# Attention and GELU layer on one core: left-over values between the first two score chunks, normalizations ahead of the sums, the last four pairs' values in the score banks

## The chip, the cores and the metric

The kernel runs on one core of a Trainium2 chip. Times are device microseconds of one execution; most executions of one kernel agree within some tenths of a per cent, this one scatters more. TensorE (PE) multiplies matrices into PSUM banks, VectorE (DVE) copies, adds and multiplies elementwise, ScalarE (ACT) takes exponentials, GpSimd (POOL) here issues transfers (and does six small instructions at the start), and SyncE (SP) issues stores and transposing transfers. A run is called slow when it took over 1.5% longer than the fastest run of the same kernel in its set; all other runs are of the fast state, and means of times are taken over these alone. Where a median or a range includes a slow run, it is said.

## The reference

```python
scores = scale * np.matmul(q, k.transpose(0, 1, 3, 2))        # 8 batches, 12 heads, 448 rows, 64 wide
m = np.max(scores, axis=-1, keepdims=True)
e = np.exp(scores - m)
attn = e / (np.sum(e, axis=-1, keepdims=True) + np.exp(-m) + 1e-09)
x = np.matmul(attn, v)              # then heads side by side: 3584 tokens x 768
h = x @ w_in                        # 768 x 2048
g = 0.5 * h * (1.0 + erf(h * inv_sqrt2))
out = g @ w_out                     # 2048 x 768
```

448 rows are three chunks of 128 and 64 left-over rows. Two heads make a pair, six pairs a batch, 48 pairs in all.

## The kernel before

Attention of later batches is woven into the two layers of earlier ones. A `step` brings the scores of one pair; in every second step (`two`) also the values of two earlier pairs; then some layer items (`work`), each of them a chain of accumulating matmuls into one bank. `ps_bank` has two banks for values and layer items alike, `ps_st` three tiles of two banks for scores.

```python
def values(g, first=True):                   # 6 matmuls, 128 rows x 64 columns of the array
    ...
    if first:
        po_t[g] = ps_bank.tile([P, 512], FP32, name="bank")
    ...
def values_left(*pairs):                     # left-over rows: 2 matmuls per pair, 64 x 64
    ...
def normalize(g):                            # VectorE: reads the pair's bank, frees it
    nc.vector.tensor_tensor(
        out=xt_t[b][:, c, :], in0=po_t.pop(g)[:, 0:S], in1=rec_t.pop(g), op=ALU.mult)

def step(s, work, late=False):
    ...
    two = s % 2 == 0 and s - 3 in et_t
    if two:
        values(s - 4)
    if s < NSTEP:
        for j in range(NK):
            scores(s, j)                     # 4 matmuls each, 64 x 64
    if two:
        values_left(s - 4, s - 3)
        normalize(s - 4)
        values(s - 3, first=False)
        normalize(s - 3)
    add_up(len(sums))                        # what is left of the denominators' additions (VectorE)
    if s < NSTEP:
        sums.extend(presum_items(s))         # 6 more
    for i, f in enumerate(work):
        ...                                  # a layer item, its copy out of the bank on VectorE
        if len(work) < 4:
            add_up((2, 4)[len(work) == 1] if i < 2 else 0)
        else:
            add_up((0, 2, 1, 1)[i])
```

The second half of batch 2's q and k is put in order by four VectorE copies into the tile `hbuf`, from which transposing transfers read; `hbuf` is later layer 1's output of batch 1. That is called after the step `r == 3` of the first batch, hence ahead of the next step's normalizations:

```python
if b == 0 and r in (-1, 3):
    c0 = 0 if r < 0 else NPAIR // 2
    for w in range(2):
        order_by_pairs(2, w, c0, c0 + NPAIR // 2)      # copies on VectorE
        transpose_on_dma(2, w, c0, c0 + NPAIR // 2)
```

The left-over rows come in four transfers per tensor and batch (`load_left`), issued by GpSimd. After the last step the last two pairs still have to go through values, denominators and normalization:

```python
load_table(SET_GELU)
values(NSTEP - 2)
values_left(NSTEP - 2, NSTEP - 1)
normalize(NSTEP - 2)
values(NSTEP - 1, first=False)
normalize(NSTEP - 1)
for f in take(2):                            # two layer-2 items, then layer 1 of the last batch
    f()
```

The softmax here doesn't subtract the row's maximum and nothing guards it: scores larger than these inputs give would overflow.

## Time and profile before

| what | before |
|---|---|
| time, median of the first 3 runs | 427.51 us (423.76 to 432.69, the highest a slow run) |
| span of the profiled run | 426.0 us |
| TensorE busy | 402.2 us (94%) |
| TensorE waits for a normalization (L414) | 6.1 us in 12 |
| TensorE waits for the last quarter of `w_out` | 4.2 us, once |
| mean clock granted to TensorE | 0.995 |

Waits are read from a list "who waited for whom: total, times, longest". An engine counts as waiting only while no instruction of its own is drawn as running. The lines themselves are in the prediction.

GpSimd's issues at the start, by start and duration:

```profile
1.99 2.63 POOL L126 DMA_DIRECT2D klraw<-in_k_dram  x4 [0.68 <-DVE oneb L180]
...
6.76 2.53 POOL L126 DMA_DIRECT2D vl<-in_v_dram  x4
...
12.87 0.72 POOL L97 DMA_DIRECT2D rawq<-in_q_dram  x1
```

Each left-over transfer occupies GpSimd 0.63 us; the first transfer of batch 1 is issued at 12.87.

### The profile page before, as it was taken

How to read it: one execution, taken by the hardware profiler on the slowest of the kernel's cores; microseconds unless marked ns; L12 is line 12 of the kernel's file. 1: busy time of each engine (PE TensorE's matmuls, PEld its weight loads, DVE VectorE, ACT ScalarE, POOL GpSimd, SP SyncE). 2: the span in 40 equal slices, each digit the busy share in tenths (PEclk: the TensorE clock that was granted, in tenths of full speed). 3: DMA queues.
4: the chain of work that ended last, by engine and by line, in shares of the span. 5: the costliest groups of instructions: out<-in, count | busy, mean ns of one | idle time of the engine just before them, and what ended most of it. 6: DMA issues, size and time to landing. Idle time of an engine off the chain costs nothing.

```text
span 426.0 us, 10972 instructions
## 1 busy us (share of the span) xinstructions
PE 402.2 (94%) x4679; PEld 260.9 (61%) x4679; DVE 199.8 (47%) x478; ACT 299.9 (70%) x450; POOL 123.7 (29%) x173
## 2 busy tenths in 40 slices
PE   6788997799999999999999999999999999999996
PEld 3345864455666666566566666656576566677785
DVE  4796435576165712575155732566056731530021
ACT  5999889397987756988687766898688676634300
POOL 8842541286540582045500563030000000000000
PEclk9999999899999999999999999999999999999999
DMA  9999999999991998169921999139011010110022
GB/s 136 149 181 204 199 176 154 194 185 164 142 113 57 143 182 69 39 102 178 114 57 39 158 143 92 58 87 155 20 38 50 27 38 2 58 38 20 2 75 74
DMA packets 137249, 43.81 MB, mean 103 GB/s; under 512 B 118320, under 2 KB 137200, under 8 KB 137200
## 3 DMA queue, kind: packets, MB, share of 16 engines
q0 software_dynamic: 92016, 22.39, 58.0%
q1 hardware_dynamic: 44400, 20.10, 25.8%
q8 instruction: 36, 0.59, 0.6%
q10 hardware_dynamic: 784, 0.62, 0.6%
q14 instruction: 13, 0.11, 0.1%
HBM read 45.61 MB, written 11.01 MB: 133 GB/s over the span
## 4 chain that ended last, share of the span: by engine, by line
PE 74%; DMA 14%; DVE 5%; POOL 3%; issue 2%; ACT 0%; DVEq 0%
PE bank L230 63%; DMA vn<-in_v_dram 5%; DMA w_in_sb<-in_moe_w_in_dram 5%; PE st L327 4%; PE bank L376 3%; DMA w_out_sb<-in_moe_w_out_dram 3%; PE st L398 2%; PE st L230 2%; DMA rawq<-in_q_dram 2%; DVE xt L414 1%; DVE ksum L361 1%; DVE osb L479 1%; DVE t L361 1%; POOL rawk L97 1%; POOL klraw L126 1%
## 5 line engine op out<-in xcount | busy, mean ns | idle before, releaser
L230 PE MATMUL bank<-xt,w_in_sb 128*64 128x448 f16 x1536 | 151.7, 353 | 1.2 <-DVE xt L414 1.1
L315 ACT ACTIVATE et<-st,expb 128x896 f16<-128x896 f32 x144 | 134.3, 1002 | 26.1 <-PE st L327 25.9
L230 PEld LDWEIGHTS <-w_in_sb 128*64 128x64 f16 x1536 | 96.2, 110 | 52.2 <-issue 5.7
L230 PE MATMUL bank<-w_out_sb,gt_odd 128*64 128x384 f16 x1024 | 88.3, 326 | 1.2 <-DVE xt L414 1.1
L479 DVE COPY osb<-bank 128x384 f32<-128x384 f32 x56 | 31.2, 558 | 123.9 <-PE bank L230 123.9
L230 PEld LDWEIGHTS <-gt_odd 128*64 128x64 f16 x1024 | 64.9, 110 | 22.9 <-issue 4.8
L230 PE MATMUL bank<-w_out_sb,gt_even 128*64 128x384 f16 x768 | 69.5, 329 | 8.0 <-DMA w_out_sb<-in_moe_w_out_dram 4.2
L230 PEld LDWEIGHTS <-gt_even 128*64 128x64 f16 x768 | 48.5, 110 | 26.9 <-issue 13.2
L414 DVE TENSOR_TENSOR xt<-bank,rec 128x448 f16<-128x448 f32 x48 | 28.8, 621 | 65.0 <-PE bank L391 61.5
L438 ACT ACTIVATE gt_odd<-bank 128x448 f16<-128x448 f32 (+1 forms) x74 | 29.2, 394 | 23.9 <-PE bank L230 22.8
L315 ACT ACTIVATE el<-st,expb 128x448 f16<-128x448 f32 x48 | 30.7, 640 | 19.2 <-PE st L398 19.2
L442 DVE COPY hbuf<-bank 128x448 f32<-128x448 f32 x54 | 33.6, 622 | 16.5 <-PE bank L230 15.7
L327 PE MATMUL st<-tqk 64*64 64x448 f16 x576 | 38.8, 362 | 2.4 <-ACT et L315 1.5
L113 POOL DMA_DIRECT2D rawq<-in_q_dram x40 | 30.7, 773 | 31.7 <-DMA vn<-in_v_dram 17.7
L361 DVE TENSOR_TENSOR ksum<-ksum,el 64x448 f16<-64x448 f16 x96 | 37.0, 385 | 2.2
L376 PE MATMUL bank<-et,vn 128*64 128x448 f16 x288 | 36.6, 361 | 0.2 <-DVE tqk L250 0.2
L97 POOL DMA_DIRECT2D vn<-in_v_dram x11 | 10.3, 933 | 90.0 <-PE bank L376 89.7
L361 DVE TENSOR_TENSOR ksum<-t,et 128x448 f16<-128x448 f16 x96 | 34.0, 384 | 1.0 <-ACT et L315 0.8
L361 DVE TENSOR_TENSOR t<-et 128x448 f16<-128x448 f16 x96 | 33.1, 386 | 1.6 <-ACT et L315 0.8
L438 ACT ACTIVATE gt_even<-bank 128x384 f16<-128x384 f32 x34 | 16.7, 491 | 21.5 <-PE bank L230 21.5
L405 ACT ACTIVATE rec<-st,oneb 128x448 f32<-128x448 f32 x42 | 26.8, 640 | 4.7 <-PE st L398 4.7
L408 ACT ACTIVATE rec<-rec 128x448 f32<-128x448 f32 x48 | 27.6, 577 | 1.5
(55 smaller groups left out, 266.1 us busy)
## 6 DMA issues: line engine op xcount, KB each, us to landing
vn<-in_v_dram POOLq DMA_DIRECT2D x6, 576.0 KB, 10.5
rawq<-in_q_dram POOLq DMA_DIRECT2D x40, 84.0 KB, 7.6
rawk<-in_k_dram POOLq DMA_DIRECT2D x32, 96.0 KB, 6.1
w_in_sb<-in_moe_w_in_dram POOLq DMA_DIRECT2D x4, 768.0 KB, 15.9
w_out_sb<-in_moe_w_out_dram POOLq DMA_DIRECT2D x4, 768.0 KB, 14.7
out_dram<-osb SPq DMA_DIRECT2D x16, 168.0 KB, 2.2
out_dram<-osb SPq DMA_DIRECT2D x16, 144.0 KB, 2.1
out_dram<-osb SPq DMA_DIRECT2D x16, 120.0 KB, 2.0
```

What stands on the lines that cost most here:

```text
L113: nc.gpsimd.dma_start(out=dst[:, :, j, e, :], in_=view[j, e])
L230: nc.tensor.matmul(out[x], lhs[:, x], rhs, start=start, stop=stop)
L315: nc.scalar.activation(out=out, in_=in_, func=AF.Exp, bias=expb, scale=scale)
L327: nc.tensor.matmul(st[cols, e, 0:S], kt[r, j, cols], qt[r], start=True, stop=True)
L361: nc.vector.tensor_tensor(out=dst, in0=a, in1=x, op=ALU.add)
L376: nc.tensor.matmul(po_t[g][e * D:(e + 1) * D, 0:S], v_t[b][:, 2 * c + e, j, :], et[:, 2 * j + e], start=(first and j == 0), stop=(not firs ...
L405: nc.scalar.activation(out=rec_t[g], in_=den_t.pop(g)[:, 0:S], func=AF.Ln, bias=oneb, scale=1.0)
L408: nc.scalar.activation(out=rec_t[g], in_=rec_t[g], func=AF.Exp, scale=-1.0)
L414: nc.vector.tensor_tensor(out=xt_t[b][:, c, :], in0=po_t.pop(g)[:, 0:S], in1=rec_t.pop(g), op=ALU.mult)
L438: nc.scalar.activation(out=dst[:, 0, :], in_=ph[:, c0:c1], func=AF.Gelu)
L442: nc.vector.tensor_copy(out=h_t[b][:, fc, :], in_=ph[:, 0:S])
L479: nc.vector.tensor_copy(out=osb, in_=po[:, 0:NHW])
```

## The change

It means to let VectorE free the value banks before TensorE needs them, to take the end's two waits away, and to shorten the stream of transfers that the start hangs on. Its core (renamed arguments cut):

```diff
 def load_left(tiles, src, b):          # batch 0: 2 transfers in place of 4
+    n = 2 if b else 1
+    for i in range(n):
...
 def step(s, work, late=False, then=None):
-    if two:
-        values(s - 4)
-    if s < NSTEP:
-        for j in range(NK):
-            scores(s, j)
-    if two:
-        values_left(s - 4, s - 3)
-        normalize(s - 4)
-        values(s - 3, first=False)
-        normalize(s - 3)
-    add_up(len(sums))
+    if s == NSTEP:
+        add_up(len(sums))
+        for g in (s - 4, s - 2):
+            st = ps_st.tile([P, 2, 512], FP32, name="st")
+            for i in range(2):
+                values(g + i, bank=st[:, i])
+        values_left(*range(s - 4, s))
+        normalize(s - 4)
+        normalize(s - 3)
+    else:
+        if two:
+            values(s - 4)
+        for j in range(NK):
+            scores(s, j)
+            if two and j == 0:
+                values_left(s - 4, s - 3)
+        if two:
+            normalize(s - 4)
+            values(s - 3, first=False)
+            normalize(s - 3)
+    if then:
+        then()                         # the reordering copies, now behind the normalizations
+    add_up(2 if two and len(work) > 3 else len(sums))
...
+            if s % 2 and i == len(work) - 1:
+                pass                   # leave the rest of the sums to the next step
-            if len(work) < 4:
+            elif len(work) < 4:
                 add_up((2, 4)[len(work) == 1] if i < 2 else 0)
             else:
-                add_up((0, 2, 1, 1)[i])
+                add_up((2, 2, 2, 0)[i] if two else (0, 2, 1, 1)[i])
...
-load_left(kl_raw, k, 2)
+nc.vector.memset(kl_raw[0], 0.0)
 ...                                    # q, k of batch 2; first half of w_out
+load_left(kl_raw, k, 2)
...
 load_table(SET_GELU)
-values(NSTEP - 2)
-values_left(NSTEP - 2, NSTEP - 1)
 normalize(NSTEP - 2)
-values(NSTEP - 1, first=False)
 normalize(NSTEP - 1)
```

More of the change, by code (lines that the diff above doesn't have):

```diff
@@ L113, in load_pairs, with left_rows @@
                 nc.gpsimd.dma_start(out=dst[:, :, j, e, :], in_=view[j, e])
-    def left_rows(c, e):
-        x = (c + e) % 2
+    def left_rows(b, c, e):
+        x = (c + e) % 2 if b else e
         return slice(x * LEFT, (x + 1) * LEFT)
     def load_left(tiles, src, b):
-        view = src[b, :, NFULL:S].rearrange("(c i e) s d -> i e s c d", i=2, e=2)
-        for i in range(2):
+        tile_, rows = tiles[b % 2], src[b, :, NFULL:S]
+        n = 2 if b else 1
+        for i in range(n):
+            dst = tile_.rearrange("p (c i) x -> p i c x", i=n)[:, i]
+            view = rows.rearrange("(c i e) s d -> i e s c d", i=n, e=2)[i]
             for e in range(2):
-                dst = tiles[b % 2].rearrange("p (c i) x -> p i c x", i=2)[left_rows(i, e), i]
                 x = slice(e * D, (e + 1) * D) if src is k else slice(0, D)
-                nc.gpsimd.dma_start(out=dst[:, :, x], in_=view[i, e])
+                nc.gpsimd.dma_start(out=dst[left_rows(b, i, e), :, x], in_=view[e])
     def load_q(b, *heads):
@@ L358, in add @@
             else:
-                r = left_rows(g % NPAIR, e)
+                r = left_rows(*divmod(g, NPAIR), e)
                 dst, a, x = sum_t[g][r, e], sum_t[g][r, e], el_t[g][r]
@@ L366, in presum_items, with values @@
         return items
-    def values(g, first=True):
+    def values(g, first=True, bank=None):
         b, c = divmod(g, NPAIR)
@@ L372, in values @@
         if first:
-            po_t[g] = ps_bank.tile([P, 512], FP32, name="bank")
+            po_t[g] = ps_bank.tile([P, 512], FP32, name="bank") if bank is None else bank
         for j in range(NK):
@@ L389, in values_left @@
             for e in range(2):
-                r = left_rows(c, e)
+                r = left_rows(b, c, e)
                 nc.tensor.matmul(
@@ L523, in add_up, with step @@
         del sums[:n]
-    def step(s, work, late=False):
+    def step(s, work, late=False, then=None):
         def middle():
@@ L633, with fetch_half @@
     add_up(4)
+    def fetch_half(b, i):
+        c0 = i * NPAIR // 2
+        for w in range(2):
+            order_by_pairs(b, w, c0, c0 + NPAIR // 2)
+            transpose_on_dma(b, w, c0, c0 + NPAIR // 2)
     def fetch(b, r):
@@ L639, in fetch @@
             load_left(vl, v, b + 2)
-        if b == 0 and r in (-1, 3):
-            c0 = 0 if r < 0 else NPAIR // 2
-            for w in range(2):
-                order_by_pairs(2, w, c0, c0 + NPAIR // 2)
-                transpose_on_dma(2, w, c0, c0 + NPAIR // 2)
+        if b == 0 and r == -1:
+            fetch_half(2, 0)
         elif b and r in (0, 1) and b + 2 < B:
@@ L665 @@
                 n = 2
-            step(s, take(n), late=(s == NSTEP or r == (2 if b else 0)))
+            step(s, take(n), late=(s == NSTEP or r == (2 if b else 0)),
+                 then=(lambda: fetch_half(2, 1)) if (b, r) == (0, NPAIR - 2) else None)
         if b == 0 and r == 0:
```

## The prediction

> **What bounds the kernel now.** I read the page's busy table first, then the list of waits of TensorE, then the timeline around the longest of them, and last the windows around the one gap that a transfer makes.
>
> ```profile
> PE 402.2 (94%) x4679; PEld 260.9 (61%) x4679; DVE 199.8 (47%) x478; ACT 299.9 (70%) x450; POOL 123.7 (29%) x173
> ```
>
> TensorE is occupied for 402.2 of 426.0 us; no other engine is near. The change neither adds nor removes a matrix multiplication, so what it can win lies in the 23.8 us in which TensorE stands still, and in what switching between kinds of multiplication costs. The waits of TensorE say who owns those gaps:
>
> ```profile
> PE bank L230 <- DVE xt L414: 6.1, 12, 1.0
> PE bank L230 <- DMA w_out_sb<-in_moe_w_out_dram: 4.2, 1, 4.2
> PE st L327 <- ACT et L315: 1.5, 3, 0.5
> PE bank L187 <- DVE klraw L174: 1.3, 1, 1.3
> ```
>
> The columns are the total, the number of waits and the longest. Twelve times the layer matmuls (L230) wait for VectorE's normalization (L414), which has to empty one of only two accumulator banks; once they wait 4.2 us for a quarter of the second weight matrix. The list restricted to 82 to 370 us gives 4.1 us in 9 waits of the first kind, and after 370 us 1.6 us in 2 (0.80 and 0.81); the twelfth, 0.38 us, lies before the transfer's wait. One typical gap in order of time (start, duration):
>
> ```profile
> 89.50 0.73 PE L376 MATMUL bank<-et,vn 128*64 128x448 f16 x6
> 89.71 0.56 DVE L479 COPY osb<-bank 128x384 f32<-128x384 f32 x1 [1.32 <-PE bank L230]
> ...
> 90.16 0.76 PE L327 MATMUL st<-tqk 64*64 64x448 f16 x12
> 90.30 0.69 DVE L361 TENSOR_TENSOR t<-et 128x448 f16<-128x448 f16 x2
> ...
> 90.76 0.36 PE L391 MATMUL bank<-el,vl 64*64 64x448 f16 x4
> 90.91 0.69 DVE L361 TENSOR_TENSOR ksum<-t,et 128x448 f16<-128x448 f16 x2
> ...
> 91.05 0.76 PE L376 MATMUL bank<-et,vn 128*64 128x448 f16 x6
> ...
> 91.51 1.15 DVE L414 TENSOR_TENSOR xt<-bank,rec 128x448 f16<-128x448 f32 x2
> ...
> 92.18 1.33 PE L230 MATMUL bank<-xt,w_in_sb 128*64 128x448 f16 x12 [0.38 <-DVE xt L414]
> ```
>
> The left-over values (L391) end by about 91.1, so the first normalization could start there; four additions (L361) stand ahead of it on VectorE and it starts at 91.51. Its bank is free at 92.13, while TensorE had been done with its own work since about 91.80. That is the 0.38 us.
>
> **The transfer.** The windows show the 4.2 us wait (engines' busy time, clock granted, share of the DMA engines, GB/s):
>
> ```profile
> 71.00:72.00 1.00, 1.00 (x16) 0.68 (x13) 0.97 (x4) 1.00 (x3) 0.00 (x0) 1.00 1.33 183
> 73.00:74.00 1.00, 0.00 (x0) 0.00 (x0) 0.00 (x0) 1.00 (x2) 0.00 (x0) 1.00 2.93 66
> 77.00:78.00 1.00, 1.00 (x11) 0.74 (x9) 0.00 (x0) 0.00 (x0) 0.00 (x0) 0.58 1.43 237
> 79.00:80.00 1.00, 1.00 (x12) 0.23 (x12) 0.97 (x4) 0.00 (x0) 0.00 (x0) 0.50 1.60 192
> ```
>
> TensorE stops at 72.25 and resumes at 76.43, and from 77 to 80.5 it gets half its clock, which costs about 1.65 us more: value, score and left-over work that takes 0.66 and 0.60 us elsewhere takes 1.31 and 1.06 here, and the rest of the layer item 0.5 us more. So all that TensorE gains before 72 us is lost again in a longer wait, unless the weights land earlier. That makes three stretches with different rules: up to 76 us (set by transfers), 76 to 369 us (TensorE and the banks), and the end.
>
> **What the Trainium skill says.** "PSUM — Partial Sum Buffer", section "PSUM bank collisions raise a hardware error", wants each bank guarded by semaphore against a second engine: the layer matmul really must wait until the normalization has read its bank. The trace agrees: TensorE resumes at 92.18, 0.05 us after the read ends. The same page, "Engine vs sequencer instructions", calls VectorE's queue strict FIFO; so additions issued earlier hold the normalization back, as the 0.4 us from 91.1 to 91.51 shows. "TensorE: Matmul & The Clock Gate", Part 1, has the clock halved after an idle window of about 3.4 us; here 4.18 us of idling brought it to 0.50 for about 3.4 us. "TensorEngine Tiling (Array Packing)", "Key Properties", says that changing the tiling mode drains TensorE: before each switch between 128*64 and 64*64 the weight loads of this trace idle 0.20 to 0.36 us. Scores and left-over values are both 64*64.
>
> **The change part by part.**
>
> 1. Left-over values move between the first and the second score chunk. Nothing is added: 4 matmuls of 0.29 us are done 8 score matmuls (8/12 of 0.60 = 0.40 us) earlier, in the same tiling mode, so no new switch. The normalization can begin about 0.4 us earlier. The price: the second bank is wanted earlier, after 0.66 us of values and 0.20 us of scores, 0.86 us after the last layer item. Above, the copy that frees it ends at 90.27, 0.77 us after 89.50. It fits, with 0.1 us to spare; where the copy is of 448 columns (mean 622 ns against 558) it is about even.
>
> 2. VectorE normalizes ahead of the sums: the instruction order of the changed kernel has the two normalizations straight after the copy, and the four t and ksum additions (4 x 0.3 us) behind them. With 1, the first normalization starts at about 90.75 in the example and ends at 91.4, against 91.80 when TensorE wants the bank: 0.4 us of slack in place of a 0.38 us gap. The postponed additions (up to 6, about 2.1 us) end some 3.1 us after the values, near the end of the first layer item (2.6 us); the copy of that item may come 0.1 to 0.5 us later, but its bank is wanted only after another item. The same move takes the four reordering copies (1.80 us, 80.38 to 82.1) from in front of the normalization at 82.03, where the gap was 1.02 us. So parts 1 and 2 take all 9 gaps from 82 to 370 us: 4.1 us.
>
> 3. The last four pairs. In the kernel before, two pairs of values run at 369.39 and two at 375.05, with these lines at the end:
>
> ```profile
> 376.33 1.04 ACT L408 ACTIVATE rec<-rec 128x448 f32<-128x448 f32 x2
> 376.94 1.16 DVE L414 TENSOR_TENSOR xt<-bank,rec 128x448 f16<-128x448 f32 x2 [1.48 <-ACT rec L408]
> 377.62 5.39 PE L230 MATMUL bank<-w_out_sb,gt_even 128*64 128x384 f16 x64 [0.81 <-DVE xt L414]
> 382.81 18.35 PE L230 MATMUL bank<-xt,w_in_sb 128*64 128x448 f16 x192
> ```
>
> From 369.39 to 382.81 are 13.42 us. Afterwards: 24 value matmuls in a row at the 98.8 ns that the 448-column layer matmuls take (151.7/1536), 2.4 us; 8 left-over ones, 0.55; three layer items at 2.6 us (the distance of the last osb copies), 7.8; four denominator matmuls, 0.4; a switch, 0.2. That is 11.35, or 2.1 us less: both gaps (1.6) and about 0.5 of switching. The score banks are free: their exponentials end near 369.0. The reciprocals of the last pairs, ready some 2.2 us after the denominators, lie beside 5.2 us of layer work.
>
> 4. Batch 0's left-over rows are fetched in 2 transfers instead of 4, for keys and for values. A transfer costs GpSimd 0.63 us to issue, so its stream runs 1.3, then 2.5 us ahead. Up to 13 us GpSimd issues without a break while the DMA engines move 136 GB/s; from 26 to 42 us they move 205. The early stretch is thus partly bound by issuing (small rows account for the rest), and I take some two thirds of 2.5 us: the last weight quarter lands 1.6 us earlier, at 74.8. The move of the next keys' left-over rows behind two weight quarters changes no bytes ahead of the last quarter. The new zeroing (0.38 us) lies before 76 us. TensorE will arrive about 1 us earlier, still wait over 3 us, and still lose its clock.
>
> Sum: 4.1 + 2.1 + 1.6 = 7.8 us; 427.5 - 7.8 = 419.7 us, or 1.8%.
>
> **The rivals.** (a) Transfers bound the early part fully: the DMA share is 1.24 from 4 to 13 us and 1.27 from 26 to 42, no lower, which speaks for it; a transfer of q issued at 9.28 that landed in 3.2 us speaks against. Then part 4 gives nothing: 421.3. (b) The weights land 2.5 us or more earlier and the wait falls well below the clock's window: 0.9 us and the 1.65 us of slow clock come on top, 417. The dip to 66 GB/s at 73 us shows that this landing is a matter of luck; it probably makes most of the spread from 423.8 to 432.7 of the kernel before. (c) A new wait replaces the old: the left-over values for their bank (0.1 us of slack), at up to 20 pair steps by 0.1 to 0.2 us, so 2 to 4 us given back, 422 to 423. (d) ScalarE becomes the bound: it idles 1.58 and 1.9 us once in a pair of steps and loses 0.4 of that; I see no room for it. Nothing points to a slower kernel.
>
> **Range and chances.** Half the uncertainty is the landing of the weights with the clock (0 to 4 us), half is rival (c) and the scatter of runs. 8 in 10: 415.5 to 424. A gain of 2% needs 8.55 us; I expect 7.8 with a spread of about 3 between kernels' means. Faster 0.42, within 2% 0.57, slower 0.01.
>
> **What would show it.** Right: the wait of L230 for L414 falls from 6.1 us to under 0.5; the additions follow the normalizations; 24 value matmuls stand in a row near the end and the layer matmuls after them have no gap; one wait for the weight transfer remains, ending at 74 to 75.5, with a dip of the clock behind it. Wrong: a wait of L391 for a copy into osb or hbuf, in each pair step; a weight wait that ends at 76 or later (part 4 void) or is gone (gain above 9 us); a gain after 82 us that differs from 6.2 us by more than 1.

## The result, and the profile after

| | before | after |
|---|---|---|
| time, median of 4 runs | 427.59 us (423.76 to 432.69, one of them slow) | 414.42 us (412.71 to 414.82) |
| mean of the fast runs | 426.3 us (3 runs) | 414.1 us (4 runs) |
| span of the profiled run | 426.0 | 410.9 |
| mean clock of that run | 0.995 | 1.000 |

Ratio of the fast runs: 0.9713, 95% interval 0.9642 to 0.9784: faster, by 2.9%, and below the range that was forecast. (A ratio here is the mean time of one kernel's fast runs over that of the other's of the same rounds, so not quite the ratio of the medians quoted.) In the changed kernel the line numbers are 3 higher: L233 are the layer matmuls, L417 the normalizations, L445 and L482 the copies out of layer banks. TensorE's busy time and its waits afterwards:

```profile
PE 396.3 (96%) x4679; PEld 245.0 (60%) x4679; DVE 199.8 (49%) x479; ACT 299.6 (73%) x450; POOL 121.1 (29%) x169
```

```profile
PE bank L241 <- DVE xt L417: 1.7, 3, 0.6
PE bank L233 <- DMA w_out_sb<-in_moe_w_out_dram: 1.5, 1, 1.5
...
PE bank L233 <- DVE hbuf L445: 0.5, 1, 0.5
```

The 6.1 us of L230 for L414 have no counterpart. The wait for weights is 1.5 us in place of 4.2. One wait is new: layer 1 of batch 1 for a copy into `hbuf`. And TensorE's busy time fell by 5.9 us although the number of matmuls is the same, 4679. Some 1.6 us of that is the slow clock of the kernel before, which stretched matmuls (worked out below); the rest is a first sign that "busy" contained waiting.

The pair step that the prediction shows, in the changed kernel (start, duration, in order of time):

```profile
82.35 0.73 PE L379 MATMUL bank<-et,vn 128*64 128x448 f16 x6
82.58 0.56 DVE L482 COPY osb<-bank 128x384 f32<-128x384 f32 x1
...
83.22 0.36 PE L394 MATMUL bank<-el,vl 64*64 64x448 f16 x4
...
83.69 0.62 DVE L417 TENSOR_TENSOR xt<-bank,rec 128x448 f16<-128x448 f32 x1 [0.55 <-PE bank L394]
...
83.89 0.76 PE L379 MATMUL bank<-et,vn 128*64 128x448 f16 x6
...
84.48 1.34 PE L233 MATMUL bank<-xt,w_in_sb 128*64 128x448 f16 x12
84.76 0.62 DVE L417 TENSOR_TENSOR xt<-bank,rec 128x448 f16<-128x448 f32 x1 [0.45 <-PE bank L379]
```

From the first value matmul to the first layer matmul: 84.48 - 82.35 = 2.13 us; before, 92.18 - 89.50 = 2.68. VectorE now waits for TensorE (0.55 us for the left-over values), not the other way round. No copy is late for the left-over matmuls: L394 stands in no line of the waits.

The wait for the last weight quarter, in windows (busy time of the engines, then clock, share of the DMA engines and GB/s at the end of the line):

```profile
70.00:71.00 1.00, 0.57 (x8) 0.22 (x3) 0.57 (x2) 1.00 (x2) 0.00 (x0) 1.00 1.39 201
71.00:72.00 1.00, 0.00 (x0) 0.00 (x0) 0.00 (x0) 1.00 (x3) 0.00 (x0) 1.00 1.46 192
72.00:73.00 1.00, 0.88 (x12) 0.77 (x13) 0.00 (x0) 0.91 (x2) 0.00 (x0) 1.00 1.40 251
```

TensorE resumes at 72.12, not 76.43, and its clock stays at 1.00. At the start GpSimd is ahead:

```profile
1.99 1.46 POOL L129 DMA_DIRECT2D klraw<-in_k_dram  x2 [0.68 <-DVE oneb L183]
...
5.55 1.37 POOL L129 DMA_DIRECT2D vl<-in_v_dram  x2
...
10.40 0.79 POOL L97 DMA_DIRECT2D rawq<-in_q_dram  x1
```

And the end is closed:

```profile
356.67 2.44 PE L379 MATMUL st<-et,vn 128*64 128x448 f16 x24
...
359.03 0.57 PE L394 MATMUL st<-el,vl 64*64 64x448 f16 x8
...
359.53 2.79 PE L233 MATMUL bank<-w_out_sb,gt_even 128*64 128x384 f16 x32
...
362.54 5.37 PE L233 MATMUL bank<-w_out_sb,gt_even 128*64 128x384 f16 x64
...
367.74 14.54 PE L233 MATMUL bank<-xt,w_in_sb 128*64 128x448 f16 x152
```

Two traces can be subtracted stretch by stretch. From 426.0 to 410.9 are 15.1 us:

| stretch | us less | how read |
|---|---|---|
| up to TensorE's resuming after the weights | 4.3 | 76.43 to 72.12 |
| resumed item and the pair step behind it | 2.8 | 1.84 + 4.44 us to 1.29 + 2.17 |
| 8 later pair steps with a listed wait | 4.4 | each 2.68 to 2.13 |
| 9 later pair steps without a listed wait | 1.7 | each 2.33 to 2.14 |
| last values to the last batch's layer 1 | 2.35 | 13.42 to 11.07 |
| new wait for `hbuf` | -0.5 | at 87.87 |

These add up to 15.05. The 2.8 are about 1.6 us of slow clock and 1.2 us of bank wait.

**The wait that the list does not show.** In nine pair steps of the kernel before TensorE had no listed wait, and yet they became shorter. One of them:

```profile
113.48 0.76 PE L376 MATMUL bank<-et,vn 128*64 128x448 f16 x6
113.59 1.39 DVE L414 TENSOR_TENSOR xt<-bank,rec 128x448 f16<-128x448 f32 x2 [9.60 <-PE bank L391]
...
114.27 1.98 PE L230 MATMUL bank<-w_out_sb,gt_odd 128*64 128x384 f16 x22
```

The first of two normalizations, 0.62 us each, runs from 113.59 to 114.21; the layer matmul starts 0.06 us later, just as in the listed cases. Six value matmuls are issued in 0.59 us (the distance in the changed kernel, 83.89 to 84.48) but drawn for 0.76, as each is drawn 0.35 us long and they overlap. A wait of 0.2 us lies under their tail.

### The profile page after: what moved, and what is told of

Same layout as the page of the kernel before. It is cut to its first block, busy times and chain, and to the rows that moved or that the text cites. A ratio compares the mean times of both kernels' runs of the same rounds, so it can differ in the third digit from the quotient of the medians.

```text
span 410.9 us, 10968 instructions
## 1 busy us (share of the span) xinstructions
PE 396.3 (96%) x4679; PEld 245.0 (60%) x4679; DVE 199.8 (49%) x479; ACT 299.6 (73%) x450; POOL 121.1 (29%) x169
## 4 chain that ended last, share of the span: by engine, by line
PE 81%; DMA 14%; POOL 3%; issue 1%; DVE 1%
PE bank L233 65%; DMA w_out_sb<-in_moe_w_out_dram 10%; PE st L330 6%; PE bank L379 6%; DMA rawk<-in_k_dram 4%; PE st L401 2%; PE st L233 2%; PE bank L394 1%; POOL vn L97 1%; POOL rawq L97 1%; PE st L379 1%; POOL vl L129 0%; POOL klraw L129 0%; POOL rawk L97 0%; DVE klraw L177 0%
## 5 line engine op out<-in xcount | busy, mean ns | idle before, releaser
L233 PE MATMUL bank<-xt,w_in_sb 128*64 128x448 f16 x1536 | 151.9, 353 | 0.5 <-DVE hbuf L445 0.5
L233 PEld LDWEIGHTS <-w_in_sb 128*64 128x64 f16 x1536 | 93.5, 110 | 54.5 <-issue 3.8
L233 PE MATMUL bank<-w_out_sb,gt_odd 128*64 128x384 f16 x1024 | 88.0, 326 | 0.0
L482 DVE COPY osb<-bank 128x384 f32<-128x384 f32 x56 | 31.2, 557 | 103.2 <-PE bank L233 103.1
L233 PEld LDWEIGHTS <-gt_odd 128*64 128x64 f16 x1024 | 57.8, 110 | 27.6 <-issue 2.1
L233 PE MATMUL bank<-w_out_sb,gt_even 128*64 128x384 f16 x768 | 68.5, 327 | 1.5 <-DMA w_out_sb<-in_moe_w_out_dram 1.5
L417 DVE TENSOR_TENSOR xt<-bank,rec 128x448 f16<-128x448 f32 x44 | 27.5, 624 | 76.1 <-PE bank L394 63.5
L233 PEld LDWEIGHTS <-gt_even 128*64 128x64 f16 x768 | 43.2, 110 | 23.8 <-issue 4.9
L330 PE MATMUL st<-tqk 64*64 64x448 f16 x576 | 41.6, 358 | 2.5 <-ACT et L318 1.5
L445 DVE COPY hbuf<-bank 128x448 f32<-128x448 f32 x54 | 33.5, 620 | 10.8 <-PE bank L233 8.9
L97 POOL DMA_DIRECT2D vn<-in_v_dram x11 | 10.5, 955 | 88.1 <-PE bank L379 85.9
L379 PE MATMUL bank<-et,vn 128*64 128x448 f16 x264 | 33.0, 356 | 0.2 <-DVE tqk L253 0.2
L330 PEld LDWEIGHTS <-tqk 64*64 64x64 f16 x576 | 15.2, 105 | 23.1 <-issue 18.7
```

Of the source, the lines that this page charges most:

```text
L97: nc.gpsimd.dma_start(out=tiles[b][:, h0:h1], in_=src[b, h0:h1, 0:n * nj].rearrange("h (p j) d -> p h j d", j=nj),)
L233: nc.tensor.matmul(out[x], lhs[:, x], rhs, start=start, stop=stop)
L330: nc.tensor.matmul(st[cols, e, 0:S], kt[r, j, cols], qt[r], start=True, stop=True)
L379: nc.tensor.matmul(po_t[g][e * D:(e + 1) * D, 0:S], v_t[b][:, 2 * c + e, j, :], et[:, 2 * j + e], start=(first and j == 0), stop=(not firs ...
L417: nc.vector.tensor_tensor(out=xt_t[b][:, c, :], in0=po_t.pop(g)[:, 0:S], in1=rec_t.pop(g), op=ALU.mult)
L445: nc.vector.tensor_copy(out=h_t[b][:, fc, :], in_=ph[:, 0:S])
```

## The experiments

Two letters tell the starting point: `a_` is the changed kernel with something undone, `b_` the kernel before with something added. Times are medians; each run is compared with runs of the kernel before on the same chip (424 to 432 us, medians 425.75 to 428.01; of these 43 runs two, at 431.52 and 432.37, were slow). The results were correct except in the two runs where a wrong result was meant. Two theories stood against each other for the 5 us more than forecast. Theory 1: the pair steps are worth more than their listed waits. Theory A: the earlier weights are worth more than 1.6 us. Rivals were that either was luck of the two traces.

### The pair step: both edits, one at a time

Left-over values behind all scores again:

```diff
-                if two and j == 0:
-                    values_left(s - 4, s - 3)
             if two:
+                values_left(s - 4, s - 3)
```

> The changed kernel with the left-over values back behind all score chunks. Theory 1 (both the place of the left-over values and the order on VectorE are needed): the first normalization can start only 0.3 us before TensorE wants its bank and takes 0.62, so each of the 19 pair steps, 2.13 us long in the changed kernel, becomes 2.3 us: about 3.5 us more, 418. Rival (the order on VectorE does it alone): pair steps stay at 2.13 to 2.15, 414.4 as the changed kernel.

Measured: 418.04 us (417.43 to 421.8). All 19 pair steps are longer than in the changed kernel, where they take about 2.13: 10 are 2.33 us and 9 are 2.40 to 2.43; yet not one line of the waits names a normalization for L233. One of the steps in this run:

```profile
108.54 0.76 PE L379 MATMUL bank<-et,vn 128*64 128x448 f16 x6
108.65 1.39 DVE L417 TENSOR_TENSOR xt<-bank,rec 128x448 f16<-128x448 f32 x2 [9.90 <-PE bank L394]
...
109.33 0.97 PE L233 MATMUL bank<-w_out_sb,gt_odd 128*64 128x384 f16 x9
```

The normalization starts as soon as the left-over values are there and ends at 109.27; TensorE starts at 109.33. So the whole loss in the pair steps, 10 x 0.20 + 9 x 0.26 = 4.3 us, is unlisted (only 0.03 and 0.10 us in each step are drawn as idle, too little for the list).

Additions ahead of the normalizations again:

```diff
-        add_up(2 if two and len(work) > 3 else len(sums))
+        add_up(len(sums))
...
-            if s % 2 and i == len(work) - 1:
-                pass
-            elif len(work) < 4:
+            if len(work) < 4:
...
-                add_up((2, 2, 2, 0)[i] if two else (0, 2, 1, 1)[i])
+                add_up((0, 2, 1, 1)[i])
```

> The changed kernel with the additions spread as in the kernel before, so that four or fewer of them stand ahead of the normalizations. Theory 1: 8 or 9 pair steps get a wait of 0.3 to 0.5 us again, the other 10 stay at 2.13: 3 to 4 us more, 418. Rival (the place of the left-over values does it alone): pair steps stay at 2.13, 414.4.

Measured: 418.54 us (417.74 to 421.85 for the three fast runs; the fourth, 425.11, was slow). The pair steps do what theory 1 says: 9 have a listed wait of 0.38 us and take 2.68, the others 2.13 to 2.15 (one stands under a slow clock). Neither edit does it alone. By the medians of fast runs this is 4.1 us over the changed kernel, by the means 5.3; 8 or 9 x 0.55 is 4.4 to 5. The traced run, at 421.85, also had a weight wait of 2.25 us with a slow clock behind it, and 1.3 us for `hbuf`.

The two edits together, on the kernel before, with copies, loads and end left alone:

```diff
                 scores(s, j)
+                if two and j == 0:
+                    values_left(s - 4, s - 3)
         if two:
-            values_left(s - 4, s - 3)
+            if s >= NSTEP:
+                values_left(s - 4, s - 3)
...
-        add_up(len(sums))
+        add_up(2 if two and len(work) > 3 else len(sums))
...
-            if len(work) < 4:
+            if s % 2 and i == len(work) - 1:
+                pass
+            elif len(work) < 4:
...
-                add_up((0, 2, 1, 1)[i])
+                add_up((2, 2, 2, 0)[i] if two else (0, 2, 1, 1)[i])
```

> The kernel before with only the two edits of the pair step: left-over values after the first score chunk, and the additions behind the normalizations (copies, loads and end as before). By the traces 8 gaps of 0.55 us and 9 hidden ones of 0.19 to 0.20 go after 82 us: 6.1 us, so 421 to 422 where the kernel before has 427.5. If only the waits that the profile lists go (8 x 0.38 = 3.0 us): 424.5.

Measured: 420.82 us (419.91 to 421.76) against 427.14; ratio 0.9844 (0.9814 to 0.9874), 6.7 us by the means of the fast runs. That is the traces' 6.1, not the listed 3.0. All pair steps but one take 2.13 to 2.15. The one exception is that behind the copies, 6.21 us with a listed wait of 3.9.

### The end

In the changed kernel the old end, with the left-over values kept between the score chunks in all other steps:

```diff
-        if s == NSTEP:
-            add_up(len(sums))
-            for g in (s - 4, s - 2):       # the four pairs' values in score banks
-                ...
-            normalize(s - 4)
-            normalize(s - 3)
-        else:
+        if True:
             if two:
                 values(s - 4)
-            for j in range(NK):
+            if s == NSTEP:
+                values_left(s - 4, s - 3)
+            else:
                 ...
...
+    values(NSTEP - 2)
+    values_left(NSTEP - 2, NSTEP - 1)
     normalize(NSTEP - 2)
+    values(NSTEP - 1, first=False)
     normalize(NSTEP - 1)
```

> The changed kernel with the last four pairs as in the kernel before. From the first of the last values to the first layer-1 matmul of the last batch: 13.4 us again instead of 11.1, 2.3 us more, 416.7. Rival (the gain at the end was lent by something else, such as an earlier arrival of the exponentials): 415 or less.

Measured: 418.33 us (417.45 to 419.55). The stretch at the end was 361.92 to 374.55, 12.6 us, so 1.6 us longer than with the new end (one of the two old gaps stays closed, as the additions no longer stand ahead of the normalizations). The other 2.3 us come from ahead of the edit: this trace waited 4.0 us for weights in two waits and 1.2 for `hbuf`. Only this one run is traced. Why all four runs of this kernel should be slower by more than the end I can't say; nothing before the last step differs.

And the new end in the kernel before, with the order inside all other steps left as it was:

```diff
+        if s == NSTEP:
+            add_up(len(sums))
+            for g in (s - 4, s - 2):
+                st = ps_st.tile([P, 2, 512], FP32, name="st")
+                for i in range(2):
+                    values(g + i, bank=st[:, i])
+            values_left(*range(s - 4, s))
+            normalize(s - 4)
+            normalize(s - 3)
+        else:
...                                    # as before
-    values(NSTEP - 2)
-    values_left(NSTEP - 2, NSTEP - 1)
     normalize(NSTEP - 2)
-    values(NSTEP - 1, first=False)
     normalize(NSTEP - 1)
```

> The kernel before with only the last four pairs' values in the score banks. From the first of these values to the last batch's layer 1: 11.1 us where it was 13.4, so 2.3 us less, 425.2. If the two gaps were not all (or came back elsewhere): off by more than 1 us.

Measured: 425.56 us (423.31 to 429.37) against 427.14; ratio 0.9971 (0.9927 to 1.0014), not resolved from 1. In the trace the stretch is 367.27 to 378.34, 11.07 us: the 2.35 us are there. The total doesn't show them clearly because the start scatters by more.

### The loads

The loads of the left-over rows as before, in the changed kernel:

```diff
-        n = 2 if b else 1              # batch 0: two transfers per tensor
-        for i in range(n):
+        for i in range(2):
...                                    # and the placing of the rows that goes with it
-    nc.vector.memset(kl_raw[0], 0.0)
+    load_left(kl_raw, k, 2)            # ahead of q, k of batch 2 and of w_out
...
-    load_left(kl_raw, k, 2)
```

> The changed kernel with the loads of the left-over rows as in the kernel before (four transfers for batch 0, the keys of batch 2 ahead of the second weight matrix). Theory A (the loads bring the last weight quarter forward by all the 4.3 us seen between the two traces): it lands at about 76.4 us again, TensorE idles 5 us and loses its clock: 4.3 + 1.6 = 6 us more, 420. Theory B (only 1.6 us of it is owed to the loads, the rest was luck of the one trace): landing at 73.7 us, 416. Theory C (all luck): 414.4.

Measured: 418.67 us (417.65 to 419.97) for the three fast runs; the fourth, 426.38, was slow, and it is the traced one, so its trace is left aside. By the means of fast runs 4.7 us over the changed kernel.

The new loads in the kernel before, the same edit the other way round:

```diff
+    n = 2 if b else 1
+    for i in range(n):
...
-    load_left(kl_raw, k, 2)
+    nc.vector.memset(kl_raw[0], 0.0)
...                                    # q, k of batch 2; first half of w_out
+    load_left(kl_raw, k, 2)
```

> The kernel before with the new loads alone. Theory A: the last weight quarter lands 4.3 us earlier, at 72.1, TensorE waits about 1 us at most and keeps its clock: 6 us gained, 421.5. Theory B: 1.6 us earlier, 426. Theory C (luck): 427.6, same as before.

Measured: 424.37 us (422.46 to 427.69) against 425.75, ratio 0.9962: no clear gain. Yet in the trace the weights came at 72.69, 3.7 us earlier than in the first trace. What took the gain is the next wait: 2.04 us for a normalization behind the four copies, and half a clock from 78.5 to 81.9 us.

Which of the two edits brings it. First, in the changed kernel, the keys' left-over rows of batch 2 early again, with two transfers kept:

```diff
     nc.vector.memset(kl_raw[0], 0.0)
+    load_left(kl_raw, k, 2)
...                                    # q, k of batch 2; first half of w_out
-    load_left(kl_raw, k, 2)
```

> The changed kernel with the keys' left-over rows of batch 2 ahead of the second weight matrix again (but two transfers for batch 0). If the order of the loads is what brings the weights forward: 417 to 419, with the weights landing at 75 or later and a wait of over 3 us. If the fewer transfers do it: 414 to 415.

Measured: 414.78 us (413.69 to 418.74). The order of the keys does not matter within the scatter.

Second, four transfers per tensor in batch 0 again, with the late keys kept (the clearing by `memset`, which four transfers don't need, goes):

```diff
-        n = 2 if b else 1
-        for i in range(n):
+        for i in range(2):
...
-    nc.vector.memset(kl_raw[0], 0.0)
...                                    # q, k of batch 2; first half of w_out
     load_left(kl_raw, k, 2)
```

> The changed kernel with four transfers each for batch 0's left-over keys and values again (but the keys of batch 2 behind two weight quarters). GpSimd issues 4 x 0.63 us more before 13 us. If the fewer transfers bring the gain: the weights land 1.5 to 2.5 us later, 416 to 419. If the order does it: 414 to 415.

Measured: 417.76 us (415.46 to 418.62), beside the changed kernel at 413.82. By the means of the fast runs 3.1 us: the fewer transfers of batch 0 bring it.

How much is scatter: two runs without any edit, to have a second trace of each kernel. The changed kernel:

> The changed kernel once more, for a second trace and the scatter. If the landing at 72.1 us was luck, it lands elsewhere by 2 us or more and the clock may be lost; the five rounds' median stays at 414 to 415.5 and the spread under 3 us.

Measured: 413.82 us (413.12 to 417.59); the weights' wait ended at 72.67. In five of its six runs the mean clock was 0.999 or 1.000, in the one at 417.59 it was 0.995.

The kernel before:

> The kernel before, once more, for a second trace of it. If the landing of the last weight quarter at 76.4 us is typical: again 75.5 to 77.5, a wait of 4 us and a dip of the clock. If it was luck: a landing anywhere from 72 to 80 us, and a time that moves with it, one to one.

Measured: 427.12 us (425.49 to 431.07), with mean clocks of 0.988, 0.988, 0.992 and once 1.000. In this trace there is no wait for the weights at all: they were there when TensorE came, at 72.7 at the latest. In its place stands a wait of 2.43 us for the normalization behind the copies, and the clock is halved behind it. So the landing at 76.4 us of the first trace was partly luck, but the time was no better for an early landing.

A steadier measure than one landing is when a given amount had been moved. Adding up the GB/s of windows of 2 us, 1.5 MB were moved by 10.8 to 11.5 us in the eight traces with four transfers (one of them, `a_old_loads`, slow), and by 9.3 to 9.7 in the twelve with two: by the means 1.6 us. For 13.25 MB, about what the last weight quarter needs, it is 73.9 to 76.6 us (mean 75.8) against 72.0 to 75.5 (mean 73.4): 2.4 us.

### Taking the weights' wait away

Layer 2 of batch 0 takes the first half's weights twice, so it never needs the last quarter. Its output is wrong, which doesn't matter for the time.

```diff
+                w0 = n0 if b else 0
...
-    po[:, 0:NHW], gt[:, fc, g0:g0 + P], w_out_sb[:, fc, n0:n0 + NHW],
+    po[:, 0:NHW], gt[:, fc, g0:g0 + P], w_out_sb[:, fc, w0:w0 + NHW],
```

First on the kernel before:

> The kernel before in which layer 2 of batch 0 takes the first half's weights twice, so that it never waits for the last weight quarter (its result is wrong on purpose). If the wait and the slow clock behind it cost 4.2 + 1.65 us: 421.7 at the median, no clock below 1.0 after 72 us. If the wait only stands in for another transfer that is late too (the values or the second half of batch 2's rows): less than 3 us gained.

Measured: 429.97 us (428.11 to 431.01) against 425.75: not 5.8 us faster but 4 slower. VectorE, in the place of the pair step behind it:

```profile
79.17 1.01 DVE L267 COPY hbuf<-rawq 112x768 f16<-112x768 f16 x2 [3.10 <-DMA rawq<-in_q_dram]
81.30 0.81 DVE L267 COPY hbuf<-rawk 128x576 f16<-128x576 f16 x2 [1.11 <-DMA rawk<-in_k_dram]
82.05 0.62 DVE L414 TENSOR_TENSOR xt<-bank,rec 128x448 f16<-128x448 f32 x1
```

The copies wait 3.1 and 1.1 us for their own rows, the normalizations stand behind them, and TensorE waits 6.4 us, until 82.72: the same moment as in the first trace of the kernel before (82.71), and with a slow clock around it, from 81.3 to 88.1 us. The wait for the weights was one of two gates in series on the same stream of transfers; opened alone it gives nothing.

The same edit on the changed kernel:

> The changed kernel with the same weights taken twice (wrong on purpose). The wait of 1.5 us goes: 412.9. The difference to b_nowait is then what the pair steps, the end and the earlier start give without any help from the weights: by the two traces 4.4 + 1.7 + 1.2 - 0.5 + 2.35 + about 1 = 10 us. If it is only 8 or less, the pair steps have been read wrongly.

Measured: 416.22 us (415.26 to 417.7). Not faster than the changed kernel either: its trace waits 2.3 us for `hbuf` and 0.85 for a sum. The difference to `b_nowait` is 13.4 us by the means, more than the 10 expected, as the kernel before still had the second gate.

### The copies

In the changed kernel the four copies ahead of the normalizations again (`fetch_half` is the changed kernel's name for copies and transposing transfers together):

```diff
-        if b == 0 and r == -1:
-            fetch_half(2, 0)
+        if b == 0 and r in (-1, 3):
+            fetch_half(2, (0, 1)[r == 3])
...
-                 then=(lambda: fetch_half(2, 1)) if (b, r) == (0, NPAIR - 2) else None)
+                 then=None)
```

> The changed kernel with the four reordering copies of batch 2's second half ahead of the normalizations again (all else as changed). Theory D (the copies, 1.8 us of VectorE and behind a transfer of their own, are a second gate right behind the weights): the first normalization ends at about 76.6 us or later, TensorE waits 1 to 2 us for it and may lose its clock for another 1 to 1.6; the 0.54 us wait for hbuf goes: 415.5 to 418. Rival (the move of the copies was worth only the 1.0 us gap of the kernel before): 414.4 to 415.

Measured: 414.27 us (413.81 to 415.3), as the changed kernel. There was a wait of 1.24 us for the normalization, but none for `hbuf`, and the clock held up in the 20 us around. The rival was right: in the changed kernel the place of the copies is worth nothing that shows.

In the kernel before the copies behind them:

```diff
             normalize(s - 3)
+        if then:
+            then()
...
-        if b == 0 and r in (-1, 3):
-            c0 = 0 if r < 0 else NPAIR // 2
-            ...
+        if b == 0 and r == -1:
+            fetch_half(2, 0)
...
-            step(s, take(n), late=(s == NSTEP or r == (2 if b else 0)))
+            step(s, take(n), late=(s == NSTEP or r == (2 if b else 0)),
+                 then=(lambda: fetch_half(2, 1)) if (b, r) == (0, NPAIR - 2) else None)
```

> The kernel before with only the copies moved behind the normalizations. Theory D: the weights still land at 75 to 77 us and the clock is still lost, so only the gap of about 1 us behind it goes: 425 to 426.5 where the kernel before has 427. Rival (the copies were the true gate and the weights only seemed so): 422 or less.

Measured: runs from 423.94 to 433.08, two of four slow. In the trace the weights' wait (4.1 us, to 77.09) and the slow clock are there, the gap behind them is not, as theory D expected.

The edits of `b_new_loads` and of `b_copies_after` together, on the kernel before (no further edit):

> The kernel before with the new loads and the moved copies together. Theory D (two gates in series: each opened alone gives 1 to 1.5 us, both together more than the sum, as the clock is then kept): 420.5 to 422. Rival (the two simply add): 423.5.

Measured: 422.66 us (421.55 to 425.9) against 426.27, ratio 0.9914 (0.9838 to 0.9989): 3.3 us by the means, where the loads alone gave 1.2 and the copies alone no verdict (two fast runs, mean 425.7 against 426.5). Mean clocks are 1.000, 1.000, 0.999 and 0.995: with both gates opened TensorE waits 1.5 and 0.4 us there in the traced run, and the clock is kept.

**When the clock is lost.** The length of a wait does not tell. In `b_new_loads` a wait of 2.04 us was followed by half a clock; in `b_end` a wait of 2.80 us in one piece was not, nor were 2.29 us in `a_nowait` and 2.22 in `a_between2`. In all 20 traces the granted clock changes on a grid of 3.41 us, which lies differently in each run. From 40 to 395 us it fell 13 times, each time after a stretch of this grid in which TensorE was drawn as busy for 1.38 us or less; after all stretches with 1.55 us or more it stayed. The stretch before the fall in `b_new_loads`, then the two that share the wait of `b_end` (busy time of PE, then clock, share of the DMA engines and GB/s):

```profile
75.09:78.50 3.41, 1.38 (x20) 1.00 1.71 188
75.43:78.84 3.41, 2.35 (x32) 1.00 1.32 250
78.84:82.26 3.42, 1.67 (x20) 1.00 1.78 207
```

So, as an estimate from these figures, a single wait of up to 3.41 - 1.55 = 1.9 us does not cost the clock wherever it falls, and the 1.5 and 1.7 us of the changed kernel's two traces are below that; between 2 and 3.4 us it depends on where the grid lies, which no edit sets. In the first 40 us the clock also fell after stretches with up to 2.1 us of busy time, which stays unexplained.

### An attempt to beat both

The four copies between the two normalizations of that step, so that `hbuf` is free earlier:

```diff
                 normalize(s - 4)
+                if then:
+                    then()
                 values(s - 3, first=False)
                 normalize(s - 3)
-        if then:
-            then()
```

> An attempt to beat both: the changed kernel with the four copies between the two normalizations of that pair step, about 1.1 us earlier. The second normalization has 2 us to spare, so nothing should wait for it; the transposing transfers that read hbuf start 1 us earlier and the 0.54 us wait of layer 1 for hbuf goes: 413.9. If the copies wait for their rows there, 414.4 or more.

Measured: 413.6 us (three runs at 413.51 to 413.65, one at 417.06).

The same kernel, to be measured beside the changed one:

> The attempt to beat both once more, beside the changed kernel on the same chip: 0.5 to 0.9 us under a_again if the earlier copies help, equal to it if the first result was scatter.

Measured: 415.08 us (413.35 to 417.83) beside the changed kernel's 413.82 in the same rounds. The first result was scatter; no gain is shown. In its trace the wait for `hbuf` is 2.2 us, longer than the changed kernel's and not gone.

### The sum of the parts

Each alone on the kernel before, by the means of fast runs: pair steps 6.7 us, loads with copies 3.3, end 1.7 (not resolved): 11.7 together. The whole change gave 428.1 to 414.3, 13.8 us, in the rounds of `a_again`. The parts are not quite additive, and one reason can be seen: with only the pair steps changed, TensorE reaches the gate behind the copies earlier and waits 3.9 us there, with a mean clock of 0.984 to 0.991 over the runs; it loses part of its gain until the gate is moved too. The rest may be scatter.

## Why the prediction was right or wrong

- **Bound and stretches: right.** TensorE bounds the kernel, what is gained before the weights' wait is lost in it, and the gains fall into start, pair steps and end.
- **Parts 1 and 2, "all 9 gaps from 82 to 370 us: 4.1 us": the mechanism right, the term mis-sized, and this is the step that failed most.** It took the listed idle time for the wait. A listed 0.38 us was 0.55 us of issue, and nine further pair steps waited about 0.2 us each without a line. By the traces it is 7.3 us (8 x 0.55 + 9 x 0.19 + 1.2); without the 1.2 us at the copies it is 6.1, and `b_order` measured 6.7 for these two edits as the only ones. The same reading made TensorE "done since about 91.80", and the slack afterwards 0.4 us: by the issue of the six matmuls it was done at 91.64 (91.05 + 0.59), and in the changed kernel the normalization ends at 84.31 (83.69 + 0.62), 0.17 us ahead of the layer matmul.
- **Part 4, "the last weight quarter lands 1.6 us earlier": somewhat small.** By bytes moved it was 1.6 us at the start and 2.4 later; the 4.3 between the first two traces contain scatter. GpSimd's issuing does bind at the start: `a_four_transfers` costs 3.1 us.
- **Part 4, "still wait over 3 us, and still lose its clock": wrong.** The wait was 1.5 us in one trace and 1.7 in the other, and the clock stayed at 1.000. This is rival (b), which the prediction named, at 417 us, but did not take as its main case. The slow clock cost about 1.6 us in the first trace. What the clock is worth over whole runs is not shown: nearly all runs of the kernel before lie at a mean clock of 0.986 to 0.996 and most of the changed kernel's at 0.999 or 1.000, but the three runs of the kernel before at 1.000 took 426.4 to 426.7 us, and seventeen at 0.992 took 424.5 to 429.7 (mean 427.2). Keeping the clock alone did not make it fast.
- **Part 3, the end, "2.1 us less": right.** 2.35 us: the stretch is 11.07 us both in the changed kernel and in `b_end`, which has the new end on the kernel before, against 13.42 before.
- **Rival (c), left-over values waiting for their bank: did not come.** No pair step of the changed kernel's two traces shows it; `a_keys_early` and `a_nowait` have one such wait each, of 0.26 us. The new wait of 0.5 us for `hbuf`, from the later copies, was not foreseen.
- **The gap of 1.0 us at the copies was read as if it were only a gap.** At a full clock it was 2.0 to 3.9 us (`b_new_loads`, `b_again`, `b_order`). In `b_new_loads` additions and copies, which don't wait for anything, are enough for 2.04 us; in `b_again` and `b_order` the copies also wait 0.3 and 3.0 us for rows of the same stream of transfers. In the first trace the weights' wait and the slow TensorE stood in front of it. The kernel before could not profit from early weights.
- **The tiling switch, "0.20 to 0.36 us before each": nearly.** It holds for 101 of the 106 switches in the trace. And the transfer of q issued at 9.28 landed after 3.1 us, not 3.2; little rests on either.

With the terms as the traces give them: pair steps 7.3 - 0.5, end 2.35, landing 2.4, clock 1.6, in sum 13.15 us. Measured were 12.2 us by the means of fast runs in the first rounds and 13.8 in those of `a_again`; 7.8 was forecast. The pair steps carry the largest part of the difference, and `b_order` shows them. The landing and the clock are read from traces, and their sum with the copies is more than the 3.3 us of `b_loads_copies`, so their sizes are not shown. What stays open is how far the loads and the place of the copies share their 3 us, as either alone lies within the scatter, and why `a_old_end` was slower at its start.

## What to carry to other kernels

Measure a wait by the distance between the issue of work on either side of it, against a place where nothing waits; the idle time drawn for a pipelined engine is shorter, and short waits vanish in it. Where several waits hang on one stream of transfers, ask what stands right behind the one that you remove, and whether an engine that frees a bank has work in its queue that waits for the same stream. Keep each wait of TensorE short: here none below 2 us cost the clock after 40 us, and longer ones did or did not, by where they fell on the clock's grid. One trace is not enough to say what the clock costs.

## What the Trainium skill lacked or had wrong

- "TensorE: Matmul & The Clock Gate", Part 1, gives an idle window of about 3.4 us as what halves the clock. Here it need not be idle: from 40 to 395 us the clock fell after each stretch of 3.41 us in which TensorE was drawn as busy for 1.38 us or less (40%), and after none with 1.55 us or more (46%). So waits of 2.04 us (`b_new_loads`), 2.25 (`a_sums_first`) and 2.43 (`b_again`) were followed by a clock of 0.50, and one of 2.80 us (`b_end`), which was split over two stretches, was not. The page gives no such share.
- "Perfetto Trace Analysis", "Identifying the Most-Contended Engine", says that matmul busy time is no good measure of how near TensorE is to its peak, as pipelined matmuls look smaller in the trace. That busy time misleads agrees, but here they look larger: six value matmuls issued in 0.59 us are drawn for 0.76. The section lacks what that does to waits: 0.17 to 0.2 us of each wait for a normalization in the pair steps lay under matmuls drawn as running, and the same 4679 matmuls were drawn as 402.2 us busy before and 396.3 after, of which the slow clock explains some 1.6 us.
